# A product and the copy behind it in two halves of 256 columns: SwiGLU on one core of Trainium2

## The chip, the cores and the metric

The kernel runs on one core of one Trainium2 chip. The metric is the device time of one execution in microseconds, the median of the runs; lower is better. The engines are called as the profile calls them: PE is TensorE (matmuls), PEld its weight loads, DVE is VectorE, ACT is ScalarE, POOL is GpSimd, SP is SyncE, which here issues DMAs.

## The reference

A causal convolution over the sequence with seven taps (softmax of a small weight, one set of taps for each of 8 heads), then RMS normalization and a SwiGLU feed-forward layer without bias, all in float32:

```python
out[s, head] = sum_k w[head, k] * x[s + k - 6, head]      # w = softmax(weight)
xn  = x / sqrt(mean(x * x) + 1e-6) * rms_g                # x: 32768 tokens, 192 wide
g   = xn @ w_gate                                         # 192 -> 1536
val = xn @ w_val                                          # 192 -> 1536
out = (g / (1 + exp(-g)) * val) @ w_out                   # 1536 -> 192
```

## The kernel before

The 32768 tokens are handled in 32 pairs of 512-token blocks (`T = 512`). Pair 0 goes through a plain path that also brings in the weights. Pairs 1 to 31 go through the class `Pair`, each with four `Unit`s (u = 0 to 3), a quarter of the 1536 hidden columns each.

Within a unit the gate and value matrices are multiplied by a fast scheme: with sums of weights (`wf`, built once) and sums of tokens (`xb`, `xc`) it needs 15 products where the plain way takes 18. A product is written (u, v, i): unit, bank role v, and which weights and which tokens. Each product is two matmuls, h = 0 (gate) on the lower 64 rows of the array and h = 1 (value) on the upper 64 rows; the two run side by side. A bank is one PSUM tile `ps0` to `ps7` of 128x512 float32. There are four for each h, handed out from the lists `free`; `Unit.new` takes one, `Unit.leave` gives it back.

The scheme needs intermediate sums of banks. `Unit.do` records the operations that make them, by letter: S copies a bank to SBUF; F ("fork") copies a bank into a new bank, on which later products go on accumulating (`FORK[2] = (4, 1)`: bank role 2 begins as a copy of role 4); N subtracts in place of a fork for h = 1; R adds a bank to a saved tile and gives the result; G is the Silu on ACT; M the multiplication of gate and value.

The order is written out by hand. `CHAINS` gives the order of the products, and the string `ORDER` puts everything else between them: `p2` is two steps of the generator `Pair.products` (so two matmuls), `AF2.0.0` is F for role 2, h = 0, unit 0 on ACT, `VN.1.0` is N for h = 1 on DVE. There is no scheduler behind it: each engine executes its instructions in the order recorded, and the framework adds the semaphore waits by tracking which tiles each one reads and writes.

In the first unit of a pair the part that matters here is

```python
# products of unit 0: (v, i) in order
4.11  1.4  5.6  4.9  0.8  5.13  4.5  1.10  0.3  4.7  5.2  2.1  4.12  3.14
"... p2 AF2.0.0 VN.1.0 AG0.0.0 p2 VR0.1.0 AF3.0.0 Dplace- AF3.1.0 p2 ..."   # from 4.7 on
```

The fourth product on role 4 is (0,4,7). For h = 0, `AF2.0.0` then copies role 4 into a new bank for role 2: an ACTIVATE of 128x512 from PSUM to PSUM (line 743). Product (0,2,1) accumulates on that copy. Between the two lies one product, (0,5,2). For h = 1, `VN.1.0` (line 814, DVE) reads role 4 instead, and (0,2,1) starts an empty bank. `AG0.0.0` is a Silu (line 839) and `AF3.0.0`, `AF3.1.0` are the two copies of role 5 into role 3, which product (0,3,14) accumulates on.

After the four units, 72 groups of small matmuls (line 934) make the output projection on four column groups of the array, in a fast scheme of its own.

Of the kernel before, what the change touches and what calls it, by code (L numbers as in the profile page):

```python
# [19 lines left out]
def kernel(  # L20
# [22 lines left out]
    T = 512  # L43
# [22 lines left out]
    XOP = (5, 6, 9, 0, 15, 14, 4, 7, 13, 10, 2, 11, 12, 8, 3)  # L66
# [11 lines left out]
    WAT = (7, 9, 2, 0, 1, 4, 5, 11, 14, 6, 10, 12, 8, 3, 13)  # L78
# [77 lines left out]
    def load(p):  # L156
# [33 lines left out]
        out=ps[6][:, 0 : H * K], lhsT=ones[:], rhs=w_row[:], start=True, stop=True,  # L190
# [11 lines left out]
    wf = [cst.tile([P, NW, P], F32, name=f"wf{u}") for u in range(NU)]  # L202
# [41 lines left out]
    def load_out(i):  # L244
# [28 lines left out]
        out=taps[:], in0=w_sb, in1=stat[:].to_broadcast([P, H, K]), op=ALU.subtract  # L273
# [7 lines left out]
        out=taps[:], in0=taps[:], in1=ssum[:].to_broadcast([P, H, K]), op=ALU.mult  # L281
# [276 lines left out]
    HALF = (LOW, UPP)  # L558
# [114 lines left out]
    def x_op(i):  # L673
        return xb[:, i // KP, i % KP, :] if i < 2 * KP else xc[:, i - 2 * KP, :]
# [54 lines left out]
    def put(at, do):  # L729
        heapq.heappush(line, (at, next(tick), do))  # L730
# [5 lines left out]
    def plus(s):  # L736
        return ALU.add if s > 0 else ALU.subtract
# [3 lines left out]
    def copy(eng, dst, src, s=1):  # L741
        if eng == "A":
            nc.scalar.activation(out=dst, in_=src, func=AF.Copy, scale=float(s))  # L743
        elif s < 0:
            nc.vector.tensor_scalar(out=dst, in0=src, scalar1=-1.0, scalar2=None, op0=ALU.mult)
        else:
            nc.vector.tensor_copy(out=dst, in_=src)
# [9 lines left out]
    CHAINS[0][5:7] = CHAINS[0][6:4:-1]  # L757
    CHAINS[0][8:10] = CHAINS[0][9:7:-1]
    CHAINS[-1][-3:] = [(NU - 1, 4, 12), (NU - 1, 2, 1), (NU - 1, 3, 14), (NU - 1, 4, 0)]
    FORK = {0: (1, 1), 2: (4, 1), 3: (5, -1)}  # L760
    RESULT = {1: ("42", -1), 0: ("41", -1), 2: ("51", -1), 5: ("44", -1), 3: ("c", 1)}

    class Unit:
# [6 lines left out]
        def new(self, v, h, product=False):  # L770
            if product and v != 5:
                i = free[h].pop(0)
            else:
                i = pick(h, not product)
            self.bk[v, h] = i
            if product:
                whole.add((h, i))
            assert (h, i) in whole
            return bank(h, i)[:]
# [9 lines left out]
                self.ht = big.tile([P, 2, NF, T], F32, name="ht")  # L789
            return self.ht[:, v // NF, v % NF, :]  # L790

        def product(self, h, v, i):
            first = (v, h) not in self.bk
            nc.tensor.matmul(  # L794
                out=self.new(v, h, True) if first else self.old(v, h),
                lhsT=wf[self.u][HALF[h], WAT[i], :], rhs=x_op(XOP[i])[HALF[h]],
                start=first, stop=True, skip_group_check=True,
            )

        def do(self, eng, act, h):  # L800
            tl, kind, v = self.tl, act[0], int(act[1:2] or 0)
            if kind == "S":
                t = tl[act[1:], h] = tiles.pop(0)
                copy(eng, t[:], self.old(v, h))
            elif kind == "F":
                src, s = FORK[v]
                copy(eng, self.new(v, h), self.old(src, h), s)
            elif kind == "D":
                b, t = self.old(5, h), tl.pop(("00", h))
                nc.vector.tensor_tensor(out=b, in0=b, in1=t[:], op=ALU.add)  # L810
                tiles.append(t)
            elif kind == "N":
                t = tl["51", h]
                nc.vector.tensor_tensor(
                    out=t[:], in0=self.old(4, h), in1=t[:], op=ALU.subtract
                )
                self.ahead = True
            elif kind == "C":
                t = tl["c", h] = tl.pop(("40", h))
                nc.vector.tensor_tensor(out=t[:], in0=self.old(5, h), in1=t[:], op=ALU.add)  # L820
            elif kind == "R":
                k, s = RESULT[v]
                if v == 2 and h and self.ahead:
                    s = 1
                t = tl.pop((k, h))
                nc.vector.tensor_tensor(  # L826
                    out=self.hv(v) if h else t[:], in0=self.old(v, h), in1=t[:], op=plus(s)
                )
                self.leave(v, h)
                if h:  # L830
                    tiles.append(t)
                else:
                    tl["g", v] = t
            elif kind == "G":
                if v in RESULT:
                    t = src = tl["g", v]
                else:
                    t, src = tiles.pop(0), self.old(v, 0)
                nc.scalar.activation(out=t[:], in_=src[:], func=AF.Silu)  # L839
                if v not in RESULT:  # L840
                    self.leave(v, 0)
                tl["g", v] = t
            else:
                t = tl.pop(("g", v))
                src = self.hv(v) if v in RESULT else self.old(v, 1)
                engine[eng].tensor_tensor(out=self.hv(v), in0=src, in1=t[:], op=ALU.mult)  # L846
                if v not in RESULT:
                    self.leave(v, 1)
                tiles.append(t)
# [24 lines left out]
    class Pair:  # L874
# [35 lines left out]

        def products(self):
            for u, v, i in itertools.chain(*CHAINS):
                for h in range(2):
                    self.units[u].product(h, v, i)
                    yield
            for form, b, lo, hi in OUTS:
                first = form in (1, 7)
                if first:
                    self.open(b, False)
                for k in range(lo, hi):  # L920
                    src, right = self.left(form, k), RIGHT[form][:, k]
                    fresh = first and k == 0
                    two = src.rearrange("p (b q e) -> p q b e", q=2, e=Q)
                    for i in range(2):
                        self.tile(b, i, 0, WIDE, right[:, i], src[:, 0:WIDE], fresh)
                    for i in range(2):
                        self.tile(b, 2 + i, 0, T // 2, right[:, 2], two[:, i], fresh)
                    yield
                    for i in range(2):
                        self.tile(b, 2 + i, T // 2, T - WIDE, right[:, i], src[:, WIDE:T], False)  # L930
                    yield
# [106 lines left out]
    def plain(hts):  # L1038


        groups = [(u, g, f) for u in range(NU) for g in (1, 0) for f in range(NF)]
        groups[0 : 2 * NF] = [(0, g, f) for f in range(NF) for g in (1, 0)]
        held = {}

        def products():
            for u, g, f in groups:
                if len(hts) <= u:
                    hts.append(big.tile([P, 2, NF, T], F32, name="ht"))
                bks = held[u, g, f] = [free[h].pop(0) for h in range(2)]
                for k in range(KP):  # L1050
                    for h in range(2):
                        nc.tensor.matmul(  # L1052
                            out=bank(h, bks[h])[:],
                            lhsT=wf[u][HALF[h], AT[h][k] * NF + f, :],
                            rhs=xb[HALF[h], g, k, :], start=(k == 0), stop=(k == KP - 1),
                            skip_group_check=True,
                        )
                yield

        def silus():  # L1060
            for i in groups:
                sg = tiles.pop(0)
                nc.scalar.activation(out=sg[:], in_=bank(0, held[i][0])[:], func=AF.Silu)
                held[i].append(sg)
                yield

        def values():
            for u, g, f in groups:
                *bks, sg = held.pop((u, g, f))
                nc.vector.tensor_tensor(  # L1070
                    out=hts[u][:, g, f, :], in0=bank(1, bks[1])[:], in1=sg[:], op=ALU.mult
                )
                tiles.append(sg)
                for h in range(2):
                    free[h].append(bks[h])
                yield

        return products(), silus(), values()

    LAG = 138  # L1080
# [87 lines left out]
    def done(it):  # L1168
# [23 lines left out]
        out=mask[:], in_=unity.rearrange("p (i h) -> p h i", h=H), axis=AX.X, op=ALU.add  # L1192
    )
    nc.vector.tensor_tensor(
        out=own[:], in0=taps[:].rearrange("p h k -> p k h"),
# [13 lines left out]
    p, sl, v = plain(hts)  # L1209
# [57 lines left out]
    for p in range(1, PAIRS + 1):  # L1267
        now = Pair(p) if p < PAIRS else None
        for w in order:
# [5 lines left out]
            eng, name = w[0], w[1:]  # L1275
# [34 lines left out]
```

## Time and profile before

| | |
|---|---|
| time, median of 3 runs | 2593.09 us (2592.47 to 2593.69) |
| profiled execution: its span, from first to last instruction; no other time of it is given | 2591.8 us |
| busy: PE, PEld | 2580.5 us, 1778.0 us |
| busy: DVE, POOL, ACT | 2298.8 us, 2190.6 us, 1553.5 us |
| line 794, products: records of 64x512 | 4960 + 2480, 591 ns each, 1214.0 + 679.7 us |
| line 743, ACT, ps<-ps of 128x512 | 558, 586 ns each |
| granted TensorE clock | 1.000 |

A float32 matmul shows as two records, one for each of its passes. The ends of matmuls are modelled: a record of a 512-column pass is normally 589 ns long and starts 429 ns after the one before it on the same rows, and a pass that has to wait shows as a longer record rather than as idle time of PE. Waits therefore show in the rows of PEld, whose load in front of a pass carries the wait. In the rows of a timeline the first number is the start in us from the start of the span, the second the time from the first start to the last end of the merged instructions, and the bracket holds the idle time before them and what ended it.

### The profile page before, as it was taken

Reading aid. Unit: us, or ns where it says so; the run is one execution under the profiler, and the core shown is the slowest. Engines: PE = TensorE matmul, PEld = TensorE weight load, DVE = VectorE, ACT = ScalarE, POOL = GpSimd, SP = SyncE. Lnnn points to the kernel's source line nnn. Section 1 sums busy time; section 2 is a strip of 40 time slices with the busy share of each in tenths; the row PEclk is TensorE's granted clock in tenths of the full one; section 3 lists DMA queues with packets and bytes.
Section 4 is the critical chain, followed back from the end, with each engine's and each line's share of the span. In section 5 each row is a group of like instructions: output and inputs, shape, how many; then the busy total and the mean of one; then the engine's idle time right before and its main releaser. Section 6 shows DMA issues by size and latency. Waiting matters only on the chain.

```text
span 2591.8 us, 60798 instructions
## 1 busy us (share of the span) xinstructions
PE 2580.5 (100%) x23872; PEld 1778.0 (69%) x23872; DVE 2298.8 (89%) x3681; ACT 1553.5 (60%) x2825; POOL 2190.6 (85%) x1791
## 2 busy tenths in 40 slices
PE   9999999999999999999999999999999999999999
PEld 6876666767667666676666676666766666766667
DVE  8898898988989989989889899899898898988975
ACT  6576555675555765556755557655566555676554
POOL 4898888988889888898888898888988888988877
PEclk9999999999999999999999999999999999999999
DMA  6232332222331323322223313233222233122210
GB/s 145 57 57 33 63 64 52 44 45 51 63 63 38 57 33 64 63 49 47 45 51 64 62 38 55 36 63 63 46 49 45 52 63 58 37 56 40 50 44 14
DMA packets 512397, 137.33 MB, mean 53 GB/s; under 512 B 483950, under 2 KB 486510, under 8 KB 512110
## 3 DMA queue, kind: packets, MB, share of 16 engines
q1 hardware_dynamic: 508364, 132.53, 27.2%
q8 instruction: 187, 3.06, 0.5%
q10 hardware_dynamic: 3746, 0.92, 0.2%
q14 instruction: 100, 0.82, 0.1%
HBM read 83.84 MB, written 49.55 MB: 51 GB/s over the span
## 4 chain that ended last, share of the span: by engine, by line
PE 99%; DVE 0%; issue 0%; DVEq 0%
PE ps L794 62%; PE ps L934 33%; PE ps L1052 2%; PE ps L1093 1%; DVE xb L647 0%; DVE wf L338 0%; DVE xc L333 0%; DVE o_sb L949 0%; DVE xc L298 0%; DVE xc L303 0%; DVE xc L306 0%; DVEq L1305 0%
## 5 line engine op out<-in xcount | busy, mean ns | idle before, releaser
L794 PE MATMUL ps<-xc,wf 64*128 64x512 f32 x4960 | 1214.0, 591 | 0.0
L794 PEld LDWEIGHTS ps<-xc,wf 64*128 64x128 f32 x4960 | 681.3, 186 | 375.3 <-issue 176.7
L794 PE MATMUL ps<-xb,wf 64*128 64x512 f32 x2480 | 679.7, 591 | 0.0
L743 ACT ACTIVATE tile<-ps 128x512 f32<-128x512 f32 x678 | 391.1, 593 | 389.0 <-PE ps L794 295.3
L743 ACT ACTIVATE tls<-ps 128x512 f32<-128x512 f32 (+1 forms) x562 | 323.5, 589 | 438.6 <-PE ps L794 222.0
L846 POOL TENSOR_TENSOR ht<-ht,tile 128x512 f32<-128x512 f32 x329 | 418.9, 1275 | 141.0 <-ACT tile L839 65.2
L794 PEld LDWEIGHTS ps<-xb,wf 64*128 64x128 f32 x2480 | 353.9, 187 | 182.9 <-issue 93.6
L846 POOL TENSOR_TENSOR ht<-ht,tls 128x512 f32<-128x512 f32 x260 | 330.6, 1274 | 86.4 <-ACT tls L839 38.8
L743 ACT ACTIVATE ps<-ps 128x512 f32<-128x512 f32 (+1 forms) x589 | 336.0, 580 | 87.9 <-PE ps L934 32.6
L962 POOL TENSOR_TENSOR early<-ht 128x512 f32<-128x512 f32 x279 | 354.8, 1276 | 4.9
L476 DVE SCALAR_TENSOR_TENSOR ps<-xh,tp,ps 128x512 f32<-128x512 f32 x450 | 320.3, 748 | 4.0 <-ACT ps L468 1.8
L934 PE MATMUL ps<-ht,wo_sb 128*32 128x128 f32 (+2 forms) x5208 | 318.5, 380 | 0.0
L934 PEld LDWEIGHTS ps<-ht,wo_sb 128*32 128x32 f32 x5208 | 233.9, 110 | 81.7 <-POOL ht L846 23.5
L934 PE MATMUL ps<-ht,x 128*32 128x128 f32 (+2 forms) x4464 | 250.7, 379 | 0.0
L826 DVE TENSOR_TENSOR tile<-ps,tile 128x512 f32<-128x512 f32 x349 | 237.4, 683 | 10.2 <-PE ps L794 5.0
L962 POOL TENSOR_TENSOR ht<-ht 128x512 f32<-128x512 f32 x186 | 239.0, 1285 | 4.9
L826 DVE TENSOR_TENSOR ht<-ps,tile 128x512 f32<-128x512 f32 x328 | 222.5, 680 | 6.5 <-ACT tile L743 6.5
L934 PEld LDWEIGHTS ps<-ht,x 128*32 128x32 f32 x4464 | 184.3, 110 | 61.3
L839 ACT ACTIVATE tile<-tile 128x512 f32<-128x512 f32 x349 | 214.5, 625 | 0.0
L826 DVE TENSOR_TENSOR ht<-ps,tls 128x512 f32<-128x512 f32 x292 | 199.0, 681 | 6.8 <-ACT tls L743 3.6
L826 DVE TENSOR_TENSOR tls<-ps,tls 128x512 f32<-128x512 f32 x271 | 184.9, 683 | 17.0 <-PE ps L794 13.8
L934 PE MATMUL ps<-early,x 128*32 128x256 f32 (+2 forms) x3348 | 196.0, 379 | 0.0
(149 smaller groups left out, 3278.1 us busy)
## 6 DMA issues: line engine op xcount, KB each, us to landing
xb<-xd SPq DMA_DIRECT2D x120, 384.0 KB
xd<-yn SPq DMA_DIRECT2D x244, 96.0 KB
xh<-in_x_dram SPq DMA_DIRECT2D x192, 105.0 KB
out_dram<-o_sb SPq DMA_DIRECT2D x122, 96.0 KB
out_dram<-o_sb SPq DMA_DIRECT2D x60, 128.0 KB
xh<-in_x_dram SPq DMA_DIRECT2D x56, 98.4 KB
out_dram<-o_sb SPq DMA_DIRECT2D x122, 32.0 KB
ht<-in_moe_w_gate_dram SPq DMA_DIRECT2D x12, 192.0 KB
```

The costliest lines, as they stand in the source:

```text
L476: nc.vector.scalar_tensor_tensor(out=dst, in0=xk, scalar=w, in1=at, op0=ALU.mult, op1=ALU.add)
L743: nc.scalar.activation(out=dst, in_=src, func=AF.Copy, scale=float(s))
L794: nc.tensor.matmul(out=self.new(v, h, True) if first else self.old(v, h), lhsT=wf[self.u][HALF[h], WAT[i], :], rhs=x_op(XOP[i])[HALF[h]], ...
L826: nc.vector.tensor_tensor(out=self.hv(v) if h else t[:], in0=self.old(v, h), in1=t[:], op=plus(s))
L839: nc.scalar.activation(out=t[:], in_=src[:], func=AF.Silu)
L846: engine[eng].tensor_tensor(out=self.hv(v), in0=src, in1=t[:], op=ALU.mult)
L934: nc.tensor.matmul(out=self.bank(b)[i * Q : (i + 1) * Q, at : at + n], lhsT=left, rhs=cols, start=fresh, stop=True, skip_group_check=True, ...
L962: engine[eng].tensor_tensor(out=dst, in0=a, in1=b, op=op)
L1052: nc.tensor.matmul(out=bank(h, bks[h])[:], lhsT=wf[u][HALF[h], AT[h][k] * NF + f, :], rhs=xb[HALF[h], g, k, :], start=(k == 0), stop=(k == ...
L1093: nc.tensor.matmul(out=bank(h, bks[h])[:, w : w + D], lhsT=hts[f // NF][HALF[h], g, f % NF, j * P : (j + 1) * P], rhs=wo_sb[HALF[h], f, :] ...
```

## The change

In unit 0 of each of the pairs 1 to 31 the two matmuls of product (0,4,7) become four: columns 0 to 255 for h = 0 and h = 1, then columns 256 to 511 for h = 0 and h = 1. The generator still has two steps for this product, so that `ORDER` keeps its places. The copy of role 4 into role 2 for h = 0 becomes two ACTIVATEs of 128x256, one for each half, one after the other in the place of the one before. Nothing else in the order of any engine changes.

```diff
+    CUT, ENDS = (0, 4, 7), (slice(0, T // 2), slice(T // 2, T))
...
-        def product(self, h, v, i):
+        def product(self, h, v, i, cols=slice(0, T)):
             first = (v, h) not in self.bk
+            to = self.new(v, h, True) if first else self.old(v, h)
             nc.tensor.matmul(
-                out=self.new(v, h, True) if first else self.old(v, h),
-                lhsT=wf[self.u][HALF[h], WAT[i], :], rhs=x_op(XOP[i])[HALF[h]],
+                out=to[:, cols],
+                lhsT=wf[self.u][HALF[h], WAT[i], :], rhs=x_op(XOP[i])[HALF[h]][:, cols],
                 start=first, stop=True, skip_group_check=True,
             )
...
             elif kind == "F":
                 src, s = FORK[v]
+                if (self.u, v) == (CUT[0], 2):
+                    to = self.new(v, h)
+                    for cols in ENDS:
+                        copy(eng, to[:, cols], self.old(src, h)[:, cols], s)
+                    return
                 copy(eng, self.new(v, h), self.old(src, h), s)
...
             for u, v, i in itertools.chain(*CHAINS):
+                if (u, v, i) == CUT:
+                    for cols in ENDS:
+                        for h in range(2):
+                            self.units[u].product(h, v, i, cols)
+                        yield
+                    continue
                 for h in range(2):
                     self.units[u].product(h, v, i)
                     yield
```

## The prediction

> **What bounds the kernel now.** I read the page first, for the busy shares and the chain that ended last.
>
> ```profile
> PE 2580.5 (100%) x23872; PEld 1778.0 (69%) x23872; DVE 2298.8 (89%) x3681; ACT 1553.5 (60%) x2825; POOL 2190.6 (85%) x1791
> ...
> PE 99%; DVE 0%; issue 0%; DVEq 0%
> PE ps L794 62%; PE ps L934 33%; PE ps L1052 2%; PE ps L1093 1%; DVE xb L647 0%; DVE wf L338 0%; DVE xc L333 0%; DVE o_sb L949 0%; DVE xc L298 0%; DVE xc L303 0%; DVE xc L306 0%; DVEq L1305 0%
> ```
>
> TensorE is the bound throughout; no other engine is late over a whole pair. So the change can only act by what it adds to the stream of matmuls or by a hole that it opens or closes there. A waiting matmul shows here as a longer one (ends are modelled), so I looked for holes with the table of windows: one window for each of three neighbouring products in the first unit of one pair, (0,4,7), (0,5,2) and (0,2,1). Its columns are the window, its length, and the busy time of PE, PEld, DVE, ACT and POOL.
>
> ```profile
> 451.37:452.22 0.86, 0.86 (x6) 0.39 (x4) 0.86 (x3) 0.12 (x1) 0.79 (x1) 1.00 1.04 133
> 452.22:453.08 0.86, 0.86 (x6) 0.22 (x4) 0.86 (x2) 0.66 (x2) 0.00 (x0) 1.00 0.86 110
> 453.08:454.02 0.94, 0.94 (x6) 0.47 (x6) 0.86 (x2) 0.94 (x2) 0.00 (x0) 1.00 0.47 95
> ```
>
> A product is two matmuls side by side (the two row halves of the array), each in two passes of 429 ns: 858 ns. Product (0,2,1), whose target is the copied bank, takes 0.94 us. The records give 78 ns too much in its first pass, in 31 of 31 pairs. The only other excess found in every pair, 104 ns at the first product, follows the change from the narrow output tiles and names no other engine. Who holds (0,2,1) is in the timelines of the weight loads and of ScalarE:
>
> ```profile
> 452.23 0.19 PEld L794 LDWEIGHTS ps<-xc,wf 64*128 64x128 f32 x2 [0.24 <-issue]
> 453.05 0.30 PEld L794 LDWEIGHTS ps<-xc,wf 64*128 64x128 f32 x4 [0.64 <-ACT ps L743]
> 453.59 0.19 PEld L794 LDWEIGHTS ps<-xc,wf 64*128 64x128 f32 x2 [0.24 <-issue]
> ```
> ```profile
> 452.42 0.58 ACT L743 ACTIVATE ps<-ps 128x512 f32<-128x512 f32 x1 [0.93 <-PE ps L794]
> 452.91 0.62 ACT L839 ACTIVATE tile<-tile 128x512 f32<-128x512 f32 x1
> 453.43 1.19 ACT L743 ACTIVATE ps<-ps 128x512 f32<-128x512 f32 x2
> ```
>
> The path is: last pass of (0,4,7) ends at 452.384 (record), the copy starts at 452.421, takes 582 ns, ends at 453.003; the weight load that waits for it starts 51 ns later, at 453.054; the first pass runs from 453.160 on, 106 ns after its load, where 453.082 was its turn. ScalarE had stood idle for 0.93 us before this copy: its length, not its queue, is on the path.
>
> **The change, part by part.**
>
> The matmuls. Two matmuls of 512 columns become four of 256: the slot of 858 ns becomes four passes of 256 columns. Passes of 256 columns in L934 follow each other at 216 ns, so 864 ns: +6 ns. Each also needs its own weight load; the L1093 group (64 rows, 192 columns, a load for each) ran 162 ns from pass to pass, so two loads per 216 ns fit. Bounds: 0 (columns alone, 429/2 each) to +10 ns. Before and after, (0,4,7) ends with its second pair of halves, lower row half included, because the order is low, high, low, high.
>
> What the first half of the copy waits for. In the order of the built program the four matmuls raise no count until the second half of the lower one; the first ACTIVATE of the copy waits for exactly that count, 425 in the first such pair, where the whole copy waited for the matmul before it was cut. The dependency is kept for the bank, not for its columns. So the first half starts no earlier than the whole copy did: 37 ns after the last pass.
>
> What the second half waits for. Its one wait is on ScalarE's own count, the one that the first half raises: it is not issued until the first has ended. What such a wait costs is in the converting stage, where L314 waits for L313 just before it: it starts 33 ns after the other's end (records; 59.82+0.61 and 60.46 in the timeline).
>
> ```profile
> 30.36 0.75 ACT L649 COPY xb<-ps 128x256 f32<-128x256 f32 x2 [1.09 <-DVE xb L647]
> ...
> 59.82 0.61 ACT L313 ACTIVATE xc<-xc,edge 128x384 uint32<-128x384 uint32 x1
> 60.46 0.61 ACT L314 ACTIVATE xc<-xc,edge 128x384 uint32<-128x384 uint32 x1
> ```
>
> How long a half takes. The bank-to-bank copy of 512 columns takes 582 ns, that of 384 columns (same line) 475 ns: 0.84 ns a column, so 256 columns take 368 ns; the L649 copies of 128x256 took 372 and those of 512 580 to 587, the same slope. Two halves held apart: 368 + 33 + 368 = 769 ns, +187 over 582. Bounds: halves of 390 ns (L617's 128-column rows take 389, but read a scale from memory, which the copy doesn't) give +231; two halves that overlap as unheld neighbours here do (445.25 to 445.73, 0.48 us from start to start for 0.59 us long, so 115 ns) give +39. I take +187, since the program's wait excludes the overlap.
>
> The Trainium skill, Perfetto Trace Analysis, Optimizing Scalar/DVE Operations, speaks for the edit: where ScalarE isn't saturated but causes bubbles on other engines, breaking up instructions may let work finish sooner. That is this case to the letter (60% busy, a bubble of 78 ns); by the rule the time would fall by up to that bubble, 31 × 78 ns = 2.4 us. The waits in the program are what I set against it; no trace so far shows a broken-up copy in this place. ScalarE: Activation LUTs, What ACT_TABLE_LOAD costs, has 186 ns + 0.833 ns an element for an ACTIVATE with immediates and 93 ns of overlap back to back; an estimate from it is 2 × 399 − 93 = 705 against 613 ns, +92 without a held second half, 31 × 92 = 2.9 us. The trace has 582 and 115 ns for 613 and 93, so the sum goes by the trace.
>
> The path then. (0,2,1) starts 6 + 187 = 193 ns later than it does now: its hole grows from 78 to about 265 ns. It has no slack left to hide any of it, since it is late already. The sum: 31 pairs × 193 ns = 6.0 us; pair 0 runs another path (L1052) and has none of it.
>
> Who stands behind. On ScalarE: the Silu at L839 and the two F3 copies for (0,3,14), all 187 ns later; (0,3,14) itself comes after (0,2,1) and so moves by 193 too, and the F3 copies keep their place before it (the upper one ends at 454.62, about 100 ns before it would be late). On TensorE: the new wait of (0,2,1) on VectorE is for a count that the copy itself already waited for; nothing. On VectorE: the subtraction at L814 waits for the upper matmul, +6 ns, and VectorE is busy until then anyway; the result from (0,2,1) comes 193 ns later, as do the products that follow. No DMA, and nothing on POOL or SP, is moved. SP's queue is the same.
>
> Made against the profiled execution: span 2591.8 + 6.0 = 2597.8 us; the runs' median is 1.3 us above that span, and I carry this over: 2599.1 us, +0.23%.
>
> **Rivals.**
> (1) It works as meant: the first half is copied while the second is multiplied. Then (0,2,1) waits only for a copy of 368 ns after the last pass: 452.384 + 0.006 + 0.037 + 0.368 + 0.051 + 0.106 = 452.952, before its turn at 453.088, and the hole is gone: 31 × (78 − 6) = 2.2 us less, 2590.9 us. It is all that can be won here. It decides if the first half starts some 430 ns before the last pass ends; the count it waits for speaks against it.
> (2) The halves are not held apart and overlap: +39 + 6 = 45 ns a pair, 1.4 us, 2594.5 us. The wait on ScalarE's own count speaks against it.
> (3) The short passes expose their weight loads: a load is 106 ns ahead of its pass when nothing hides it, so two further loads bared a pair add 2 × 106 × 31 = 6.6 us, 2605.7 us. The 162 ns passes of L1093 speak against it.
> (4) The delay brings a second hole, at (0,3,14), because the F3 copies fall behind: up to another 187 ns, 5.8 us, 2604.9 us; it needs them to slip by 100 ns more than the matmuls do.
>
> **How the numbers follow.** About 0.2% (5.2 us, 167 ns a pair) is what a measurement of this kernel can tell from no change. My forecast: 0.86; as meant: 0.03; overlapping halves: 0.06; the two dearer ones together: 0.05. The forecast's own terms run from 180 to 220 ns a pair in what I believe of them, 5.6 to 6.8 us, and the three runs spread by 0.6 us either way, so 2598.0 to 2600.6; the dearer half of 390 ns (+237 with the passes, 7.3 us) takes the top to 2601.0, and a little lost in the irregular holes of single pairs takes the bottom to 2597.4. With rivals beyond both ends, that leaves under 2 in 10 outside. Faster by over 0.2% is closed to every case, as the hole is worth 2.4 us: 0.01. Within 0.2%: rivals 1 and 2 and the low tail of the forecast, below 167 ns a pair, 0.14. Slower: 0.85.
>
> **What the profile after should show.** On ScalarE a pair of ACTIVATE ps<-ps of 128x256, 62 in all, about 368 ns each, 0.40 us from start to start, the first one beginning some 37 ns after the last pass of (0,4,7). The weight load of (0,2,1) idle for about 0.8 us in place of 0.64, released by ACT. The window of (0,2,1) about 1.12 us in place of 0.94, those of (0,4,7) and (0,5,2) still 0.86, and the interval from pair to pair 79.55 us in place of 79.36. I am wrong if the first half starts before the last pass of (0,4,7), if the two overlap, or if the new time lies anywhere but in front of (0,2,1).

## The result and the profile after

The changed kernel takes 2598.77 us (median of 13 runs, 2598.05 to 2599.45) against 2593.09 us (13 runs): 5.7 us more, a ratio of 1.0021 with a 95% interval of 1.0014 to 1.0028. It is slower by 0.2%, or 183 ns for each of 31 pairs; the forecast was 2599.1 us.

The page of the changed kernel has the same engine as the bound. PE is busy 5.9 us longer, which with modelled ends is the longer hole; PEld, whose loads run beside the matmuls, is busy 46.7 us longer; DVE, ACT and POOL differ by 2.1 us at most:

```profile
span 2597.6 us, 61108 instructions
...
PE 2586.4 (100%) x23996; PEld 1824.7 (70%) x23996; DVE 2298.5 (88%) x3681; ACT 1555.6 (60%) x2856; POOL 2190.7 (84%) x1791
```

The table of windows, over the same three products (0,4,7), (0,5,2) and (0,2,1) of pair 4:

```profile
372.58:373.44 0.86, 0.86 (x10) 0.78 (x8) 0.86 (x3) 0.12 (x1) 0.80 (x1) 1.00 1.06 134
373.44:374.30 0.86, 0.86 (x6) 0.19 (x2) 0.86 (x2) 0.63 (x2) 0.00 (x0) 1.00 0.44 61
374.30:375.43 1.12, 1.12 (x6) 0.49 (x6) 0.86 (x2) 1.12 (x4) 0.09 (x1) 1.00 0.49 100
```

The cut product is hardly longer than the whole one (0.863 us in the records, for 0.858). Nearly all that is new stands in the third window, 1.12 us for 0.94. The same stretch in the timelines of ScalarE and of the weight loads:

```profile
373.64 0.77 ACT L743 ACTIVATE ps<-ps 128x256 f32<-128x256 f32 x2 [0.94 <-PE ps L796]
374.32 0.62 ACT L846 ACTIVATE tile<-tile 128x512 f32<-128x512 f32 x1
374.84 1.07 ACT L743 ACTIVATE ps<-ps 128x512 f32<-128x512 f32 x2
```
```profile
372.58 1.06 PEld L796 LDWEIGHTS ps<-xc,wf 64*128 64x128 f32 x10 [0.17 <-issue]
374.46 0.30 PEld L796 LDWEIGHTS ps<-xc,wf 64*128 64x128 f32 x4 [0.82 <-ACT ps L743]
375.00 0.19 PEld L796 LDWEIGHTS ps<-xc,wf 64*128 64x128 f32 x2 [0.23 <-issue]
```

ScalarE waited as long as before (0.94 us against 0.93): the first half did not begin while TensorE was still at the product. In the records the last short pass ends at 373.605 and the first half starts at 373.642, 37 ns later; it takes 368 ns, the second follows 400 ns after the first one's start, which is 32 ns after its end, and also takes 368. So the copy takes 768 ns for 582. The weight load of (0,2,1) comes 52 ns after that and its first pass 106 ns later. Its turn was 374.303, it starts at 374.568: a hole of 265 ns, in every pair, where it had been 78.

The chain in order of time gives the step from pair to pair:

```profile
205.72 52.12 PE ps L796 x244
257.83 27.44 PE ps L947 x337
285.27 52.11 PE ps L796 x244
```

From 205.72 to 285.27 is 79.55 us. The same rows of the kernel before:

```profile
205.53 51.92 PE ps L794 x240
257.45 27.44 PE ps L934 x337
284.89 51.92 PE ps L794 x240
```

From 205.53 to 284.89 is 79.36 us. The median step grew by 195 ns: 187 are the longer hole, 5 the passes, and 3 come in the stretch of the output projection and were not followed.

### The profile page after: what moved, and what is told of

Same layout as the page of the kernel before. It is cut to its first block, busy times and chain, and to the rows that moved or that the text cites. A ratio compares the mean times of both kernels' runs of the same rounds, so it can differ in the third digit from the quotient of the medians.

```text
span 2597.6 us, 61108 instructions
## 1 busy us (share of the span) xinstructions
PE 2586.4 (100%) x23996; PEld 1824.7 (70%) x23996; DVE 2298.5 (88%) x3681; ACT 1555.6 (60%) x2856; POOL 2190.7 (84%) x1791
## 4 chain that ended last, share of the span: by engine, by line
PE 99%; DVE 0%; issue 0%; DVEq 0%
PE ps L796 62%; PE ps L947 33%; PE ps L1065 2%; PE ps L1106 1%; DVE xb L647 0%; DVE wf L338 0%; DVE xc L333 0%; DVE o_sb L962 0%; DVE xc L298 0%; DVE xc L303 0%; DVE xc L306 0%; DVEq L1318 0%
## 5 line engine op out<-in xcount | busy, mean ns | idle before, releaser
L796 PE MATMUL ps<-xc,wf 64*128 64x512 f32 (+1 forms) x5084 | 1226.8, 582 | 0.0
L796 PEld LDWEIGHTS ps<-xc,wf 64*128 64x128 f32 x5084 | 715.7, 186 | 346.9 <-issue 124.3
L796 PE MATMUL ps<-xb,wf 64*128 64x512 f32 x2480 | 686.6, 591 | 0.0
L796 PEld LDWEIGHTS ps<-xb,wf 64*128 64x128 f32 x2480 | 364.6, 187 | 171.9 <-issue 76.3
L743 ACT ACTIVATE ps<-ps 128x512 f32<-128x512 f32 x620 | 338.1, 558 | 86.6 <-PE ps L947 32.6
```

The lines of the kernel that those rows point to most:

```text
L796: nc.tensor.matmul(out=to[:, cols], lhsT=wf[self.u][HALF[h], WAT[i], :], rhs=x_op(XOP[i])[HALF[h]][:, cols], start=first, stop=True, skip_ ...
```

## The experiments

The theory: the cost is the copy of bank 4, longer because it is made of two ACTIVATEs that are held apart, and the copy cannot begin sooner since dependencies are kept for the whole bank. The rivals: the short passes bare their weight loads; two instructions cost two fixed times, held or not; a dependency by columns is there but something else hid the gain.

**The product alone** (the whole copy is restored in `Unit.do`):

```diff
-                if (self.u, v) == (CUT[0], 2):
-                    ...
                 copy(eng, self.new(v, h), self.old(src, h), s)
```

> Only the product (0,4,7) is cut; the copy stays whole. Theory (the time is the two held halves of the copy): the four short passes take 863 ns for 858, +5 ns a pair, 0.15 us in all: 2593.2 us, and the hole in front of (0,2,1) stays near 78 ns. Rival (short passes bare their weight loads): most of the 5.7 us of the whole change are here, 2598 to 2599 us.

2594.0 us against 2593.28 us of the kernel before on the same chip, ratio 0.9999 (0.9990 to 1.0009): the medians lie 0.7 us apart, and the interval includes no difference. The product and (0,2,1) in the table of windows:

```profile
450.32:451.18 0.86, 0.86 (x10) 0.78 (x8) 0.86 (x3) 0.12 (x1) 0.79 (x1) 1.00 1.00 127
452.04:452.98 0.94, 0.94 (x6) 0.47 (x6) 0.86 (x2) 0.94 (x2) 0.00 (x0) 1.00 0.48 96
```

The hole is the old one, and the median step is 79.367 us, 8 ns more. The matmuls' side of the change costs 0.2 us by the trace, which is too little for the runs to show. The rival of the bared loads falls.

**The copy alone** (the product stays whole):

```diff
-                if (u, v, i) == CUT:
-                    ...
                 for h in range(2):
                     self.units[u].product(h, v, i)
```

> Only the copy is cut; the product stays whole. Theory: 368 + 32 + 368 ns for 582 ns, +186 ns a pair, 5.8 us: 2598.6 to 2598.9 us, hole of about 264 ns, as with the whole change. Rival (short passes): 2593.1 us.

2598.89 us against 2593.28 us, ratio 1.0023 (1.0014 to 1.0032). The window of (0,2,1):

```profile
453.33:454.46 1.12, 1.12 (x6) 0.49 (x6) 0.87 (x2) 1.12 (x4) 0.09 (x1) 1.00 0.44 87
```

It again takes 1.12 us, the hole is again 265 ns, the step 79.550 us. The copy alone makes nearly the whole loss, and the two parts add up to within 4 ns (191 + 8 ns against 195 for both).

**The halves not held apart:**

```diff
-                    for cols in ENDS:
-                        copy(eng, to[:, cols], self.old(src, h)[:, cols], s)
+                    copy(eng, spill[:], self.old(src, h)[:, ENDS[0]], s)
+                    copy(eng, to[:, ENDS[1]], self.old(src, h)[:, ENDS[1]], s)
```

> As the whole change, but the first half of the copy is written to a scratch tile in SBUF, so that the second half no longer waits for it (columns 0 to 255 of the copied bank are left out of the computation). Two ACTIVATEs of 256 columns as before, without the wait between them. Theory (the wait that holds them apart bars the overlap of about 115 ns and adds 32 ns): second half starts about 0.26 us after the first instead of 0.40, hole about 130 ns, +55 ns a pair, 1.7 us: 2594.8 us. Rival (two instructions cost two fixed times whether held or not): second half 0.37 to 0.40 us after the first, 2598 us or more.

2595.84 us against 2593.28 us, ratio 1.0010 (1.0000 to 1.0019): 2.6 us by the medians, less than half of the loss, though there are as many ACTIVATEs on as many elements. The timeline of ScalarE:

```profile
453.25 0.38 ACT L743 ACTIVATE spill<-ps 128x256 f32<-128x256 f32 x1 [0.94 <-PE ps L798]
453.53 0.38 ACT L743 ACTIVATE ps<-ps 128x256 f32<-128x256 f32 x1
453.83 0.61 ACT L848 ACTIVATE tile<-tile 128x512 f32<-128x512 f32 x1
```

Second start 280 ns after the first (records) where it was 400. The overlap is 103 ns, not the 115 I had from 512 columns, and the halves last 383 and 379 ns, not 368; so the pair of them takes 659 ns, 77 more than the whole copy. With the passes that is 82 ns a pair, 2.5 us, as measured (the step, 79.444 us, grew by 85 ns); the expected 1.7 us was too low by these two. The wait is what holds the two apart: without it the copy is 109 ns shorter. What is left, 77 ns, is the price of two instructions rather than one.

The scratch tile also moves the first half's destination from PSUM to SBUF. That is not what lets the two overlap: in the kernel before, the two copies of role 1 into role 0 (`AF0.1.0`, `AF0.0.0`) go from PSUM to PSUM, the second without a wait, and it starts 89 to 92 ns before the first has ended in all 31 pairs. In this row they last 606 and 575 ns and together 1.09 us:

```profile
445.73 1.09 ACT L743 ACTIVATE ps<-ps 128x512 f32<-128x512 f32 x2
```

**Four pieces of the copy** (product whole; `ENDS` are four slices of 128 columns):

```diff
-    CUT, ENDS = (0, 4, 7), (slice(0, T // 2), slice(T // 2, T))
+    CUT, ENDS = (0, 4, 7), [slice(k, k + T // 4) for k in range(0, T, T // 4)]
```

> The product whole, the copy in four pieces of 128 columns. Theory: 4 x 261 + 3 x 32 = 1140 ns for 582, +558 ns a pair, 17.3 us: 2610.4 us; hole of about 636 ns. A cost by elements alone with one fixed time would give 2593 to 2594 us; overlapping pieces (115 ns each, no wait) 4 x 261 - 3 x 115 = 699 ns, +117 a pair, 2596.7 us.

2610.18 us against 2593.28 us, ratio 1.0064 (1.0049 to 1.0079): 16.9 us. On ScalarE:

```profile
453.43 1.14 ACT L743 ACTIVATE ps<-ps 128x128 f32<-128x128 f32 x4 [0.93 <-PE ps L796]
```

1.14 us, as the theory has it, pieces of 262 ns with 31 to 32 ns between them, a hole of 639 ns. From 262 and 368 ns the price is 0.83 ns a column and about 155 ns a piece, plus the 32 ns of the wait: each further held cut costs some 187 ns.

**The order that would overlap.** In `ORDER` the step of (0,4,7) is the `p2` ahead of `VR1.1.0`; `AF2.0.0` stands behind the step after it, (0,5,2), and the excerpt in the section on the kernel begins there. So both halves of the product are recorded ahead of both halves of the copy. Here the first half of the copy is recorded between the halves of the product (E is a new letter for it; F makes only the second half):

```diff
-... AS51.0.0 VR1.0.0 p2 VR1.1.0 VR0.0.0 p2 AF2.0.0 VN.1.0
+... AS51.0.0 VR1.0.0 p1 AE2.0.0 p1 VR1.1.0 VR0.0.0 p2 AF2.0.0 VN.1.0
...
+            elif kind == "E":
+                src, s = FORK[v]
+                copy(eng, self.new(v, h)[:, ENDS[0]], self.old(src, h)[:, ENDS[0]], s)
```

> The whole change, but the first half of the copy is recorded between the two halves of the product, so that it waits for the first halves alone; the order of work that the cut would need to overlap. Theory (dependencies are kept for the whole bank, so the second halves of the product then wait for that copy): the first copy starts 0.4 us earlier, but TensorE stands still in front of the second halves for 37 + 368 + 52 + 106 ns after the last pass of the first ones, a hole of about 720 ns, while the hole at (0,2,1) closes (-78): +650 ns a pair, 20 us: about 2613 us. Rival (dependencies by columns; the copy is hidden): the hole closes, 2591 us.

2612.93 us against 2593.42 us, ratio 1.0074 (1.0061 to 1.0088): 19.5 us, with a step of 80.010 us, 651 ns more. Weight loads and ScalarE:

```profile
453.52 0.19 PEld L796 LDWEIGHTS ps<-xc,wf 64*128 64x128 f32 x2 [0.17 <-issue]
454.56 0.73 PEld L796 LDWEIGHTS ps<-xc,wf 64*128 64x128 f32 x8 [0.85 <-ACT ps L743]
```
```profile
454.15 0.37 ACT L743 ACTIVATE ps<-ps 128x256 f32<-128x256 f32 x1 [0.50 <-PE ps L796]
455.30 0.37 ACT L743 ACTIVATE ps<-ps 128x256 f32<-128x256 f32 x1 [0.79 <-PE ps L796]
```

The first copy now does start after the first halves alone, ScalarE having waited 0.50 us instead of 0.94. But the weight load of the second halves, which write other columns of the bank it reads, is released by that copy: (0,4,7) takes 727 ns more than the whole product did, and there is no hole at (0,2,1). Product and copy take turns on the bank, whichever is recorded first. Whether the chip itself would let them work on it at the same time was not tried; the waits are put in by the framework. Nor was a version tried in which each half of the product has a PSUM tile of its own.

**A product more of cover, with the whole copy and with the halves.** Product (0,0,3) goes behind (0,4,7), so that two products lie between it and (0,2,1); both kernels are changed alike:

```diff
-    CHAINS[0][8:10] = CHAINS[0][9:7:-1]
...
-... p2 VR1.1.0 VR0.0.0 p2 AF2.0.0 VN.1.0 AG0.0.0 p2 VR0.1.0 AF3.0.0 Dplace- AF3.1.0 p2
+... p2 VR1.1.0 VN.1.0 VR0.0.0 p2 AF2.0.0 AF3.0.0 p2 VR0.1.0 AF3.1.0 Dplace- AG0.0.0 p2
```

> The kernel before, whole product and whole copy, but product (0,0,3) is moved behind (0,4,7), so that two products (1716 ns) lie between it and (0,2,1); on VectorE N comes before R0, on ScalarE the two F3 copies before the Silu. Theory (the copy's length is on the path only by 78 ns a pair): the hole is gone, 31 x 78 = 2.4 us less, 2590.7 us, unless the Silu, 1.6 us later, is missed by GpSimd. Rival (TensorE's stream is bound elsewhere, the hole only moves): 2593.1 us.

> The changed kernel with the same new order. Theory: the held halves take 768 ns and have 858 ns more cover than needed before, so they cost nothing: only the short passes' +5 ns a pair remain over the kernel with the new order alone, 2590.9 us. Rival (halves cost ScalarE time that is missed anywhere later): 2593 us or more.

2604.59 us with the whole copy and 2605.58 us with the halves, against 2593.42 us: ratios 1.0043 (1.0030 to 1.0056) and 1.0046 (1.0033 to 1.0060). The times missed what I expected by 14 and 15 us, but not for the reason the pair was made for. The hole at (0,2,1) is gone in both, and the median step is 79.742 and 79.748 us: in the regular step the cut product and copy cost 6 ns once something covers them, against 195 without. That explains 0.2 of the 1.0 us between the two medians; in the two profiles another 0.4 us lies ahead of pair 1 and 0.4 us in holes of single pairs, and why all five runs with the halves took longer than all five with the whole copy stays open. What both lose against the kernel before is lost elsewhere; the weight loads of the first of the two:

```profile
450.68 0.19 PEld L793 LDWEIGHTS ps<-xb,wf 64*128 64x128 f32 x2 [0.23 <-issue]
451.53 0.29 PEld L793 LDWEIGHTS ps<-xc,wf 64*128 64x128 f32 x2 [0.65 <-ACT tls L743]
452.05 0.18 PEld L793 LDWEIGHTS ps<-xc,wf 64*128 64x128 f32 x1 [0.22 <-DVE tls L747]
...
457.84 0.51 PEld L793 LDWEIGHTS ps<-xb,wf 64*128 64x128 f32 x4 [0.35 <-ACT tls L743]
```

The loads at 451.53 and 452.05 are those of (0,4,7), for h = 0 and h = 1. The move has taken a product away in front of them, and there they now wait for the saves of bank 4 (`AS42.0.0`, `VS42.1.0`) that must be made before the bank goes on accumulating: 181 ns in the steps from pass to pass, both row halves taken together. The load at 457.84 is that of (0,4,0), in the next unit; it waits for a later save of the same bank, `AS44.0.0`, which costs another 211 ns. A further 68 ns come in the stretch of the output projection and were not followed. Less the 78 ns won at (0,2,1), that is the step's 383 ns to within 1. Bank 4 is read by a copy after each of its products; here, moving cover to one of them took it from another.

**The product in four** (four matmuls of 128 columns for each row half, the copy whole):

```diff
-                    for cols in ENDS:
+                    for n, cols in enumerate(ENDS):
                         for h in range(2):
                             self.units[u].product(h, v, i, cols)
-                        yield
+                        if n % 2:
+                            yield
```

> The product cut in four matmuls of 128 columns for each row half, the copy whole. Theory: a pass of 128 columns lasts 107 ns and its weight load is 106 ns ahead of it, so eight passes take about 870 ns for 858, +10 to +20 ns a pair: 2593.4 to 2593.7 us. Rival (loads are bared when passes are short): 8 passes at the 162 ns of the 192-column passes, 1300 ns, +440 ns a pair, 2606 us.

2594.06 us against 2593.42 us, ratio 1.0002 (0.9993 to 1.0011); the step is 34 ns longer, 1.1 us in all. The product in the table of windows:

```profile
450.56:451.45 0.89, 0.89 (x18) 0.89 (x16) 0.89 (x3) 0.12 (x1) 0.81 (x1) 1.00 0.95 121
```

Eight passes take 891 ns, 111 each, and PEld is busy for all of the 0.89 us (0.78 with halves), which suggests that here the loads begin to set the pace; no run separates this from a cost of each pass. The 33 ns are above my 10 to 20 and far from the rival's 440.

## Why the prediction was right, by its steps

- **The bound, and the hole of 78 ns as what can be won.** Right: 78 ns in every pair before, and the two kernels with cover have no hole there.
- **The passes, +6 ns.** Measured: 863 for 858 ns, +5.
- **What the first half waits for.** Right: it starts 37 ns after the last pass of the whole product, as the whole copy did. The order with the first copy between the halves shows the reason from the other side.
- **What the second half waits for.** Right: 32 ns after the first one's end (33 forecast). That the wait costs the overlap, and is more than half of the loss, is shown by the halves that are not held.
- **The length of a half, 368 ns.** Measured 368, in all 62. The copy takes 768 ns (769 forecast), the hole is 265 ns (265), (0,2,1) takes 1.12 us (1.12), the step is 79.55 us (79.55).
- **Who stands behind.** Nothing new was late: no hole follows at (0,3,14), and rival 4 did not come.
- **The sum.** 31 × 193 ns = 6.0 us was forecast. The traces have 31 × 195 ns = 6.0 us in the regular steps, and the spans differ by 5.8 us (2597.6 − 2591.8): what the 30 steps show above their median, in single pairs, sums to 1.1 us in the profile before and 0.7 us in the one after. These 0.4 us were not worked out in the forecast; only the bottom of its range allowed for them. The medians differ by 5.7 us. One term around the sum was off: what lies outside the span is 1.8 us in the profiled run of the changed kernel (2599.39 − 2597.6), not 1.3. The 1.3 came from setting a span of one execution against the median of others, and it fell out of the difference.

The Trainium skill's sentence in Perfetto Trace Analysis, Optimizing Scalar/DVE Operations, that breaking up instructions may let work finish sooner, has its condition met here (ScalarE 60% busy, a hole of 78 ns) and its result not: the product was broken up too, and still the first piece could not start sooner, since its wait is for the whole bank. The first paragraph of that section gives each Scalar operation an overhead of its own and says that larger operations can help if the engine is saturated; the runs show such an overhead, about 155 ns a piece, on a ScalarE that is not saturated. The 93 ns of overlap that ScalarE: Activation LUTs, What ACT_TABLE_LOAD costs, has for neighbours is 103 ns in the run of the halves that are not held, and is lost altogether to a neighbour's wait; its 0.833 ns an element agrees with 262 and 368 ns for 128 and 256 columns.

No experiment points to a version that beats both kernels. At best 2.4 us (0.09%) could be had at this place, and every form of the cut copy that was tried takes longer than the whole one.

## What to carry to other kernels

Before a step is cut to overlap it with the next, read in the order of the built program which count each piece waits for: here the first piece waited for all of the producer and the second for the first piece, and then the cut can only lengthen the path. A held piece on the path costs its fixed time and the gap of its wait, 155 + 32 = 187 ns here for each cut; two halves that were not held cost 77 ns over the whole copy. Off the path the cut product and copy added 6 ns to the step. And where every product on a bank has just enough cover, moving cover to one can uncover another, as it did here.

## What the runs showed of the hardware

- Weight loads of 64x128 keep up with passes of 256 columns (216 ns a pass, PEld busy 0.78 of 0.86 us). With 128 columns PEld is busy throughout and a pass takes 111 ns, 4 more than a quarter of 429.
- The same 256-column ACTIVATE from PSUM takes 368 ns when it is held back until its neighbour has ended and 379 ns when it overlaps with it, 103 ns of them.
- Two PSUM-to-PSUM ACTIVATEs of 512 columns with no wait between them overlap by some 91 ns; one that waits for its neighbour on the same engine starts 32 ns after that one's end.
